# Token sums of a seven-product matrix scheme, made from resident token tiles instead of a second load, with a new instruction order

## The chip, the cores and the metric

The kernel runs on one core of one Trainium2 chip. TensorE (PE in the profile) multiplies matrices, VectorE (DVE) and ScalarE (ACT) work elementwise, GpSimd (POOL) and SyncE (SP) mostly issue DMA transfers. The metric is the device time of one execution in microseconds (us).

## The reference

Two branches work on the same 2048 tokens of 512 features and are mixed by a gate per token.

```python
g = sigmoid((x * gate_w).sum(-1, keepdims=True))
X = rfft2(x);  a = irfft2(X * (w_r + 1j * w_i), (2048, 512))     # a spectral filter
h = gelu(einsum("bsd,df->bsf", x, w1) + b1)                      # 512 -> 1792
b = einsum("bsf,fd->bsd", h, w2) + b2                            # 1792 -> 512
out = g * a + (1 - g) * b
```

Inputs are `x` (1, 2048, 512), `w1` (512, 1792), `w2` (1792, 512), the filter (2048, 257), all float32.

## The kernel before

Products in full float32 accuracy are made of rounded parts: an operand is split into a high part `h` (ScalarE copies it to the rounded type) and a low part `l` (VectorE subtracts `h` from the operand), and three products hh, hl, lh are added up on TensorE.

The tokens are taken in four classes `c` (position modulo 4, after a reordering), 512 tokens each. Classes 0 and 1 (`CA`) are the first half, 2 and 3 (`CB`) the second. The transform reads the tokens in 16 tiles of 128 x 512 (`xf`, tile `j` belongs to class `j % 4`); `forward(j)` folds a tile (`eo`, `w`), multiplies it with cosines and sines (`pd`, with the gate's weights in two extra columns of the table `cf`), splits the result (`zb`), and multiplies with twiddle tables `tf` (`py`). For the first half's classes `forward` also calls `split_x`, which writes the high and low part of the tile for the dense branch.

The dense branch takes 14 blocks of 128 hidden features. Blocks 0 and 1 of the first half are done with plain products (`ph`, in `plain`). All others go in pairs through `seven`: a 2 x 2 block product made with seven half-size products instead of eight (the banks `nu` and `ux`). It needs, besides some token blocks themselves, four sums and differences of them: with the four blocks 11, 12, 21, 22 (feature half by class) these are

```python
t1 = x12 - x11;  t3 = x22 - x12;  t2 = x22 - t1;  t4 = x21 - t2
```

and sums of weights (`spread_w`). After the activation the second product adds into the banks `po`, whose running sums `s` are kept in SBUF between groups of blocks.

In the kernel before, `spread_x("A")` loads the tokens of the first half a second time, in another layout (`xc`, 8 transfers of 256 KB into `xbA`), makes the four combinations with VectorE and splits each. `spread_x("B")` does so for the second half, where all seven forms are made from the loads.

The order of all work is a table, `ORDER`: the functions add numbered steps to a graph, and the steps are emitted in the order of the table, each to its engine's queue, which runs in order. A second table, `SLOTS`, says which buffer slot each tile takes. The numbers `more=` in the calls only describe costs for making the table and emit nothing.

Names in the order and the profile: `xA..` are split token forms of the first half, `xAt..` split combinations, `wa`, `wb` weights of blocks 0 and 1 and of the second product, `wA` weights of the seven-product scheme, `none` fillers that multiply zeros (nine at the start, five later), `gb` the gate spread to 512 columns per class.

Of the kernel before, what the change touches and what calls it, by code (L numbers as in the profile page):

```python
# [16 lines left out]
P = 128  # L17
# [332 lines left out]
def tile_kernel(ctx: ExitStack, tc: tile.TileContext, xt, xc, w1, w2, b1, b2, x0g, wf, wrev, out, consts):  # L350
# [193 lines left out]
    def new_forms(s, ks):  # L544
        FX.update(((s, k), buf("xhl", [P, 2, 2, 4 * P], F32R, f"x{s}{k}", parts=16, cls="xf")) for k in ks)

    def piece(b, hl, e, js=range(4)):
        return [(b, 8 * hl + 4 * i + j) for i in e for j in js]
# [18 lines left out]
    def forward(j):  # L567
# [13 lines left out]
        if c in CA:  # L581
            if j < 4:
                new_forms("A", ("11", "21") if c == 0 else ("12", "22"))
# [646 lines left out]
```

## Time and profile before

| | us |
|---|---|
| median of 3 runs | 358.27 |
| lowest and highest | 358.09, 358.92 |
| the profiled execution | 357.73 |
| its span, first to last instruction | 355.8 |

The page's rows give, for each engine, busy time, share of the span and number of instructions; PEld is TensorE's loading of weights, which overlaps the products. In rows of a timeline the first two numbers are start and duration in us, and a bracket at the end says how long the engine idled before and what ended the wait. Rows of stretches give for each engine the busy time and number of instructions, then TensorE's granted clock, the share of the DMA engines' time, and GB/s. The clock is at 1.00 in nearly all of the span.

### The profile page before, as it was taken

How to read it: one execution, taken by the hardware profiler on the slowest of the kernel's cores; microseconds unless marked ns; L12 is line 12 of the kernel's file. 1: busy time of each engine (PE TensorE's matmuls, PEld its weight loads, DVE VectorE, ACT ScalarE, POOL GpSimd, SP SyncE). 2: the span in 40 equal slices, each digit the busy share in tenths (PEclk: the TensorE clock that was granted, in tenths of full speed). 3: DMA queues.
4: the chain of work that ended last, by engine and by line, in shares of the span. 5: the costliest groups of instructions: out<-in, count | busy, mean ns of one | idle time of the engine just before them, and what ended most of it. 6: DMA issues, size and time to landing. Idle time of an engine off the chain costs nothing.

```text
span 355.8 us, 5738 instructions
## 1 busy us (share of the span) xinstructions
PE 348.8 (98%) x1770; PEld 294.8 (83%) x1770; DVE 323.1 (91%) x674; ACT 294.8 (83%) x612; POOL 38.7 (11%) x52
## 2 busy tenths in 40 slices
PE   7999999999999999999999999999999999999995
PEld 5988888888887888888888888878888888888884
DVE  5999997799999999999999999999989987779856
ACT  4989999999999984996678894589999899999510
POOL 1011101000102200010000400003000000021230
PEclk9999999999999999999999999999999999999999
DMA  7999868937798959997888954479403347345598
GB/s 230 371 270 321 158 191 287 242 125 212 184 277 210 332 115 294 357 272 236 282 274 224 220 110 99 131 261 207 135 7 104 96 134 234 123 106 133 111 201 272
DMA packets 47790, 72.47 MB, mean 204 GB/s; under 512 B 5648, under 2 KB 19472, under 8 KB 47760
## 3 DMA queue, kind: packets, MB, share of 16 engines
q1 hardware_dynamic: 40480, 61.51, 53.0%
q0 software_dynamic: 6848, 10.27, 18.5%
q10 hardware_dynamic: 432, 0.33, 0.3%
q8 instruction: 14, 0.23, 0.2%
q14 instruction: 16, 0.13, 0.1%
HBM read 52.55 MB, written 19.41 MB: 202 GB/s over the span
## 4 chain that ended last, share of the span: by engine, by line
PE 88%; DMA 5%; ACT 3%; DVE 1%; SPq 1%; issue 1%; DVEq 0%; ACTq 0%
PE po L415 39%; PE uxB L415 11%; PE uxA L415 9%; PE nuB L415 8%; PE nuA L415 7%; PE pz L415 4%; PE pa L415 3%; PE pd L415 3%; PE py L415 3%; DMA xbA<-in_xc 2%; DMA wb3l_raw<-in_w 2%; DMA xf<-in_xt 1%; PE ph L415 1%; ACT s L942 1%; DMA xf<-in_x0g 1%
## 5 line engine op out<-in xcount | busy, mean ns | idle before, releaser
L932 ACT ACTIVATE po<-s 128x512 f32<-128x512 f32 (+1 forms) x49 | 28.8, 594 | 8.0 <-DVE t L962 7.4
L424 ACT ACTIVATE s<-po 128x512 f32<-128x512 f32 x40 | 23.8, 597 | 13.1 <-PE po L415 12.8
L794 ACT ACTIVATE sw<-y,al 64x512 f32<-64x512 f32 x32 | 22.5, 718 | 0.5
L755 DVE TENSOR_TENSOR m<-y,wf 128x514 f32<-128x514 f32 x32 | 21.3, 688 | 0.6
L415 PEld LDWEIGHTS pd<-cf,w 128*128 128x128 f32 x128 | 17.7, 190 | 3.7 <-DVE cf L529 2.2
L415 PE MATMUL pd<-cf,w 128*128 128x129 f32 x128 | 19.2, 276 | 1.5 <-DVE cf L529 1.4
L415 PE MATMUL py<-zb,tf 128*128 128x258 f32 x96 | 19.6, 292 | 0.1
L409 POOL DMA_DIRECT2D w<-bacc x8 | 9.6, 1256 | 91.3 <-DVE w L842 81.0
L415 PEld LDWEIGHTS pz<-tg,pq 128*128 128x128 f32 x128 | 17.5, 190 | 1.9 <-issue 0.3
L415 PE MATMUL pz<-tg,pq 128*128 128x128 f32 x128 | 18.6, 275 | 0.0
L415 PEld LDWEIGHTS py<-zb,tf 128*128 128x128 f32 x96 | 15.5, 189 | 2.6 <-ACT zb L608 0.3
L801 DVE SCALAR_TENSOR_TENSOR pq<-y,al,sw 128x256 f32<-128x256 f32 x32 | 15.1, 478 | 2.8 <-ACT sw L794 1.9
L415 PE MATMUL nuB<-xB,wB0h 128*128 128x512 f32 x56 | 17.4, 391 | 0.0
L415 PE MATMUL pa<-zb,ci 128*128 128x256 f32 x96 | 16.2, 290 | 0.0
L415 PEld LDWEIGHTS pa<-zb,ci 128*128 128x128 f32 x96 | 14.0, 189 | 1.7 <-DVE zb L814 0.2
L612 DVE TENSOR_TENSOR zb<-pd,zb 128x256 fp32r<-128x256 f32 x32 | 13.2, 418 | 2.1 <-ACT logit L611 2.0
L415 PE MATMUL nuA<-xA,wA0h 128*128 128x512 f32 x48 | 14.9, 392 | 0.0
L942 ACT ACTIVATE s<-po,b2t 128x512 f32<-128x512 f32 x16 | 10.6, 689 | 5.0 <-PE po L415 5.0
L632 ACT ACTIVATE y<-pys 64x257 f32<-64x257 f32 x32 | 13.0, 416 | 0.8 <-DVE pys L629 0.3
L575 DVE TENSOR_TENSOR eo<-xf 128x256 f32<-128x256 f32 x32 | 12.6, 417 | 0.8 <-DMA xf<-in_x0g 0.4
L608 ACT ACTIVATE zb<-pd 128x256 fp32r<-128x256 f32 x32 | 11.9, 387 | 1.5 <-PE py L415 0.9
L814 DVE TENSOR_TENSOR zb<-pz,zb 128x512 fp32r<-128x512 f32 x16 | 10.9, 686 | 2.0 <-ACT zb L813 2.0
(532 smaller groups left out, 1225.3 us busy)
## 6 DMA issues: line engine op xcount, KB each, us to landing
wf<-in_wf SPq DMA_DIRECT2D x16, 257.0 KB, 3.9
xf<-in_xt SPq DMA_DIRECT2D x14, 256.0 KB, 5.0
tf<-tf SPq DMA_DIRECT2D x16, 192.0 KB, 3.6
wrA<-in_w SPq DMA_DIRECT2D x12, 256.0 KB, 5.5
xbA<-in_xc SPq DMA_DIRECT2D x8, 256.0 KB, 4.2
xbB<-in_xc SPq DMA_DIRECT2D x8, 256.0 KB, 4.8
bacc<-s SPq DMA_DIRECT2D x8, 256.0 KB, 2.8
w<-bacc POOLq DMA_DIRECT2D x8, 256.0 KB, 4.5
```

What stands on the lines that cost most here:

```text
L415: pe.matmul(ps, w, x, start=start, stop=stop, **more)
L424: a(lambda: act.activation(o.ap(), i.ap(), AF.Copy, scale=scale), n, [i], [o])
L575: v(lambda s=s, op=op: vec.tensor_tensor(eo.ap()[:, s], x.ap()[:, 0:2], x.ap()[:, 2:4], op=op), 256, [x], [(eo, s)])
L608: a(lambda c=c: act.activation(segs(xh, c), both(c), AF.Copy), 256, [ps[c]], [(xh, c)])
L612: v(lambda c=c: vec.tensor_tensor(segs(xl, c), both(c), segs(xh, c), op=ALU.subtract), 256, [ps[c], (xh, c)], [(xl, c)])
L632: a(lambda o=o, i=i: act.activation(Y[j].ap()[o:o + HP, 1], pys.ap()[i:i + HP, 1], AF.Copy), 257, [(pys, 1)], [(Y[j], 1 + k)], more=0.1)
L755: v(lambda mk=mk, k=k, y=y, w=w: vec.tensor_tensor(mk.ap(), y.ap(), w.ap()[:, k:k + 1, :ND].to_broadcast([P, 2, ND]), op=ALU.mult), 514, [ ...
L794: a(lambda sw=sw, y=y, o=o, i=i: act.activation(sw.ap()[o:o + HP], y.ap()[i:i + HP, ::-1, :HD], AF.Copy, scale=al.ap()[i:i + HP, 0:1]), 51 ...
L801: v(lambda sw=sw, pq_=pq_, y=y, j=j, k=k, op=op: vec.scalar_tensor_tensor(pq_.ap()[:, k], y.ap()[:, k, :HD], al.ap()[:, 1 + j:2 + j], sw.a ...
L814: v(lambda n=n, ps=ps: vec.tensor_tensor(zl.ap()[:, :, :, n], ps.ap(), zh.ap()[:, :, :, n], op=ALU.subtract), 512, [ps, (zh, n)], [(zl, n)])
L932: a(lambda ps=ps, n=n, o=o: act.activation(ps.ap(), o.ap()[:, n], AF.Copy), size, [o], [ps])
L942: a(lambda o=o, ps=ps, q=q: act.activation(o.ap(), ps.ap(), AF.Identity, bias=b2t.ap()[:, q:q + 1]), 600, [b2t, ps], [o])
```

## The change

`spread_x("A")` and its eight loads are gone. A new function `spread_a`, called from `forward` for each tile of class 1, makes the four combinations from the token tiles of class 0 and class 1 that the transform has loaded (kept in `RAW`), and splits them. The split forms of the first half are laid out in pairs: one buffer holds the high parts of two forms, another the low parts (`new_pair`), so that a split of a tile is one ScalarE instruction of 512 columns and one VectorE instruction of 512, where it was two and two of 256; two tiles of class 0 keep two ScalarE-side instructions of 256. The readers (`plain`, `seven`) take the forms through a function that says which buffer and part to read. `ORDER` and `SLOTS` are new throughout, which moves instructions on every engine.

```diff
-    def split_x(c, x, j1):
+    def split_x(pair, x, j1, first=False):
         n = slice(j1 * P, (j1 + 1) * P)
-        for k in range(2):
-            b = FX["A", ("11", "21")[k] if c == 0 else ("12", "22")[k]]
...
-                a(lambda b=b, k=k: act.activation(b.ap()[:, 0, :, n], x.ap()[:, 2 * k:2 * k + 2], AF.Copy), 256, i, o)
-        for k in range(2):
...
-            v(lambda b=b, k=k: vec.tensor_tensor(b.ap()[:, 1, :, n], x.ap()[:, 2 * k:2 * k + 2], b.ap()[:, 0, :, n], op=ALU.subtract), 256,
-              [*i, *piece(b, 0, range(2), [j1])], piece(b, 1, range(2), [j1]))
+        h, l = pair
...
+        else:
+            a(lambda: act.activation(h.ap()[:, :, n], x.ap(), AF.Copy), 512, [x, gate], where(h, range(2)))
+        v(lambda: vec.tensor_tensor(l.ap()[:, :, n], x.ap(), h.ap()[:, :, n], op=ALU.subtract), 512, [x, *where(h, range(2))], where(l, range(2)))
+
+    XP, RAW = {}, ([], [])
+
+    def spread_a(j1):
+        if j1 == 0:
+            XP["t1"], XP["t2"] = (new_pair("A", ks) for ks in (("t1", "t3"), ("t2", "t4")))
+        x, y = RAW[0][j1], RAW[1][j1]
+        t, u = (buf("w", [P, NQ, P], F32, f"xt{k}{j1}", parts=2, cls="xt") for k in range(2))
+
+        def less(o, n, i, k, w, m):
+            v(lambda: vec.tensor_tensor(o.ap()[:, 2 * n:2 * n + 2], i.ap()[:, 2 * k:2 * k + 2], w.ap()[:, 2 * m:2 * m + 2], op=ALU.subtract),
+              256, [i if i in (x, y) else (i, k), w if w in (x, y) else (w, m)], [(o, n)])
+
+        less(t, 0, y, 0, x, 0)
+        less(t, 1, y, 1, y, 0)
+        less(u, 0, y, 1, t, 0)
+        less(u, 1, x, 1, u, 0)
+        split_x(XP["t1"], t, j1)
+        split_x(XP["t2"], u, j1)
@@ in forward
-            split_x(c, x, j // 4)
+            split_x(XP[c], x, j // 4, c == 0 and j < 8)
+            RAW[c].append(x)
+            if c:
+                spread_a(j // 4)
@@ at the program's end
     group("A", 0)
-    spread_x("A")
@@ ORDER, first line of 110
-17 14 10 21 22 8 11 16 9 15 0 2 1 60 33 29 28 24 23 30 25 26 31 57 495 27 56 39 35 3 37 38 40 4 58 492 59 490 491 493
+10 21 22 14 8 18 20 19 17 11 9 0 1 2 3 4 5 6 7 32 60 59 33 513 514 528 106 16 15 28 29 23 24 31 26 56 55 25 57 30 27
```

TensorE's queue at the program's start, before:

```order
L415 MATMUL none_92<-zero_90 128x512 x9
L415 MATMUL pd01_124<-cf_86,w0_113 128x129
L415 MATMUL none_92<-zero_90 128x256
L415 MATMUL pd00_128<-cf_86,w0_113 128x129 x2
L415 MATMUL pd01_124<-cf_86,w0_113 128x129
L415 MATMUL none_92<-zero_90 128x256 x2
L415 MATMUL pd41_155<-cf_86,w4_133 128x129 x2
L415 MATMUL ph0_1_160<-xA11_104,wa1h_152 128x256 x2
L415 MATMUL ph0_1_160<-xA21_106,wa1h_152 128x256 x2
L415 MATMUL ph0_0_176<-xA11_104,wa0h_139 128x128 x2
```

The same queue and place, now:

```order
L414 MATMUL none_94<-zero_90 128x512 x9
L414 MATMUL none_94<-zero_90 128x256 x5
L414 MATMUL ph0_1_118<-xA11_21h_109,wa1h_116 128x256 x4
L414 MATMUL pd00_144<-cf_125,w0_133 128x129 x2
L414 MATMUL pd40_148<-cf_125,w4_140 128x129 x2
L414 MATMUL pd41_153<-cf_125,w4_140 128x129 x2
L414 MATMUL pd01_156<-cf_125,w0_133 128x129
L414 MATMUL ph0_0_164<-xA11_21h_109,wa0h_162 128x128 x4
L414 MATMUL py0_189<-zb1_76,tf0_167 128x258 x2
```

The five fillers come all at once, and four `ph` products of block 1 stand ahead of the first `pd`.

SyncE's queue of transfers at the start, before (`war` are the raw weights behind `wa`, `al` a small table of the last stage):

```order
L504 DMA xf4_84<-in_xt 128x256
L509 DMA cf_86<-cf 128x258
L504 DMA xf4_84<-in_xt 128x256
L509 DMA cf_86<-cf 128x258
L872 DMA war1_120<-in_w1 128x512
L869 DMA war0_135<-in_w1 128x256 x2
L534 DMA al_145<-al 128x17
L477 DMA xf8_147<-in_xt 128x512
L412 DMA tf4_183<-tf 128x384
L412 DMA tf0_188<-tf 128x384
L477 DMA xf12_193<-in_xt 128x512
```

and now:

```order
L503 DMA xf4_87<-in_xt 128x256 x2
L898 DMA war1_114<-in_w1 128x512
L533 DMA al_123<-al 128x17
L508 DMA cf_125<-cf 128x258 x2
L895 DMA war0_158<-in_w1 128x256
L411 DMA tf0_167<-tf 128x384
L895 DMA war0_158<-in_w1 128x256
L476 DMA xf12_171<-in_xt 128x512
L476 DMA xf8_173<-in_xt 128x512
L476 DMA xf9_181<-in_xt 128x512
L1048 DMA wrA4_185<-in_w1 128x512
```

`war1` and the second half of tile 4 moved ahead of the table `cf`, one `tf` moved ahead and the other behind, and a weight of the seven-product scheme (`wrA4`) came in among the token tiles.

ScalarE's queue in the opening, behind the first split of weights, before:

```order
L560 ACTIVATE xA21_106<-xf4_84 128x2x128
L560 ACTIVATE xA11_104<-xf0_78 128x2x128
L608 ACTIVATE zb1_80<-pd00_128 128x256
L560 ACTIVATE xA21_106<-xf8_147 128x2x128
L611 ACTIVATE logit_167<-pd00_128 128x2
L608 ACTIVATE zb1_80<-pd01_124 128x2x128
L560 ACTIVATE xA11_104<-xf8_147 128x2x128
```

and now:

```order
L634 ACTIVATE zb0_82<-pd40_148 128x256
L634 ACTIVATE zb1_76<-pd00_144 128x256
L568 ACTIVATE xA11_21h_109<-xf8_173 128x4x128
L637 ACTIVATE logit_209<-pd00_144 128x2
L634 ACTIVATE zb0_82<-pd41_153 128x2x128
L568 ACTIVATE xA11_21h_109<-xf12_171 128x4x128
L423 ACTIVATE wA0h2_240<-wrA4_185 128x512
L568 ACTIVATE xA12_22h_246<-xf9_181 128x4x128
L637 ACTIVATE logit_209<-pd41_153 128x2
L634 ACTIVATE zb1_76<-pd01_156 128x2x128
```

Splits of whole token tiles and of one weight block (`wA0h2`) now stand ahead of the copy of `pd01`.

More of the change, by code (lines that the diff above doesn't have):

```diff
@@ new lines, in new_form, with new_pair @@
+    def new_form(s, k):
+        b = buf("xhl", [P, 2, 2, 4 * P], F32R, f"x{s}{k}", parts=16, cls="xf")
+        FX[s, k] = lambda i, e: (lambda: b.ap()[:, i, e], [(b, 8 * i + 4 * e + j) for j in range(4)])
+    def new_pair(s, ks):
+        x = [buf("xhl", [P, 4, 4 * P], F32R, f"x{s}{'_'.join(ks)}{i}", parts=16, cls="xf") for i in "hl"]
+        for n, k in enumerate(ks):
+            FX[s, k] = lambda i, e, n=n: (lambda: x[i].ap()[:, 2 * n + e], [(x[i], 8 * n + 4 * e + j) for j in range(4)])
+        return x
@@ new lines, in split_x, with where @@
+    def split_x(pair, x, j1, first=False):
+        n = slice(j1 * P, (j1 + 1) * P)
+        h, l = pair
+        def where(b, ks):
+            return [(b, 4 * q + j1) for k in ks for q in (2 * k, 2 * k + 1)]
+        if first:
+            for k in range(2):
+                s, i = slice(2 * k, 2 * k + 2), [(x, k), gate]
+                if j1 == 0 and k:
+                    v(lambda s=s: vec.tensor_copy(h.ap()[:, s, n], x.ap()[:, s]), 256, i, where(h, [k]))
+                else:
+                    a(lambda s=s: act.activation(h.ap()[:, s, n], x.ap()[:, s], AF.Copy), 256, i, where(h, [k]))
+        else:
+            a(lambda: act.activation(h.ap()[:, :, n], x.ap(), AF.Copy), 512, [x, gate], where(h, range(2)))
+        v(lambda: vec.tensor_tensor(l.ap()[:, :, n], x.ap(), h.ap()[:, :, n], op=ALU.subtract), 512, [x, *where(h, range(2))], where(l, range(2)))
@@ L977, in last @@
                 store(lambda s=s, i=i, w=w: sp.dma_start(dst[:, n.start + i:n.start + i + w], t.ap()[:, s]), w / 2, o, [])
-    def put(b, e, x):
-        h, l = ((lambda i=i: b.ap()[:, i, e]) for i in range(2))
-        a(lambda: act.activation(h(), x.ap(), AF.Copy), 512, [x], piece(b, 0, [e]))
-        v(lambda: vec.tensor_tensor(l(), x.ap(), h(), op=ALU.subtract), 512, [x, *piece(b, 0, [e])], piece(b, 1, [e]))
-    def less(o, x, y):
-        v(lambda: vec.tensor_tensor(o.ap(), x.ap(), y.ap(), op=ALU.subtract), 512, [x, y], [o])
@@ L1072, in emit @@
                     for wi, xi in ((0, 0), (0, 1), (1, 0)):
-                        mm(o.ap(), w(wi, e), x.ap()[:, xi, e], start and k == 0, k == 5, skip_group_check=not start)
+                        mm(o.ap(), w(wi, e), x(xi, e)[0](), start and k == 0, k == 5, skip_group_check=not start)
                         k += 1
-            m(emit, 512, 6, [*bs, x], [o])
+            m(emit, 512, 6, [*bs, *[p for i in range(2) for e in range(2) for p in x(i, e)[1]]], [o])
         def plus(o, i, t):
@@ L1169, in tile_kernel @@
         stage4(c)
-    spread_x("B")
+    spread_x()
     for p in range(len(GROUPS[1])):
```

67 lines of the change are left out of this document (29 added, 38 removed), and 197 rows, old and new, of tables (ORDER, SLOTS).

## The prediction

> **What bounds the kernel now.** I read the page's engine shares first, then the busy time by stretches, then the chain that ended last, then the timelines of TensorE, VectorE, ScalarE and SyncE for the opening.
>
> ```profile
> span 355.8 us, 5738 instructions
> PE 348.8 (98%) x1770; PEld 294.8 (83%) x1770; DVE 323.1 (91%) x674; ACT 294.8 (83%) x612; POOL 38.7 (11%) x52
> 0.00:20.00 20.00, 17.43 (x117) 15.62 (x118) 15.69 (x50) 13.33 (x43) 2.66 (x13) 1.00 0.90 305
> 110.00:260.00 150.00, 149.87 (x661) 123.58 (x660) 145.69 (x279) 122.38 (x234) 17.93 (x21) 1.00 0.78 215
> 118.60 19.07 PE po L415 x84
> ```
>
> TensorE is busy 98% of the span. That alone proves little, since pipelined matmuls overlap in the records; the two other lines do. In the stretch from 110 to 260 us it issued 661 records in 150 us, 0.227 us each, and the chain has 84 `po` matmuls in 19.07 us, again 0.227. So TensorE never waited there: 0.227 us is its own pace for 512 columns, and no order of the other engines can make this stretch shorter, only longer. VectorE had 145.69 of 150 us busy beside it, so it is the engine with the least to spare (4.3 us).
>
> The Trainium skill ("Trainium Kernel Development and Optimization", Best Practices) says to judge the distance to the limit by the share of weight loading, not by matmul busy time. By that, 83% would leave some 60 us to win. The trace differs: in the stretch without a single wait weight loading is also only 123.58 of 150 us (82%), so 83% is here what a full TensorE looks like, and I go by the pace of the matmuls.
>
> What can be won lies at the two ends. Of TensorE's opening:
>
> ```profile
> 1.05 4.21 PE L415 MATMUL none<-zero 128*128 128x512 f32 x9 [1.05 <-DVE zero L483]
> 6.70 0.49 PE L415 MATMUL pd<-cf,w 128*128 128x129 f32 x2 [1.44 <-DVE cf L529]
> 14.12 0.65 PE L415 MATMUL ph<-xA,wa1l 128*128 128x256 f32 x4
> 14.60 0.28 PE L415 MATMUL py<-zb,tf 128*128 128x258 f32 x1
> 21.27 0.40 PE L415 MATMUL py<-zb,tf 128*128 128x258 f32 x2
> 21.51 0.62 PE L415 MATMUL ph<-xA,wa1h 128*128 128x512 f32 x2
> 27.10 1.05 PE L415 MATMUL pd<-cf,w 128*128 128x129 f32 x8
> 27.91 0.61 PE L415 MATMUL py<-zb,tf 128*128 128x258 f32 x3
> ```
>
> From starts to starts: four 256-column matmuls take 0.48 us (14.12 to 14.60), so 0.12 each; two of 258 columns 0.24, so 0.12 each; eight `pd` records, which are four fold instructions, 0.81, so 0.20 a fold. Half of 0.12 for 128 columns is an estimate. Before the first 512-column `ph` matmul at 21.51 the kernel before has, behind the nine warm-ups, 5 fillers (0.60), 44 `ph` of 256 (5.28), 8 of 128 (0.48), 23 `py` (2.76) and 20 folds (4.05): 13.2 us. With 1.05 and 4.21 that is 18.4, so 3.1 us of the opening were waiting.
>
> **The change, part by part.**
>
> *TensorE's work.* Counted by tile and width in the two orders, every group is the same (`po`, `nu`, `ux`, `ph`, `py`, `pd`, `pz`, `pa`, fillers). Cost 0; the span can move only by waits.
>
> *Loads removed.* Eight `xbA` loads of 256 KB leave SyncE's queue.
>
> ```profile
> L993 SPq DMA_DIRECT2D xbA<-in_xc x8: 328/426/777, 11.6 to 43.0; - x8
> L981 ACT ACTIVATE xAt<-xbA x8: 622/648/673, 37.6 to 53.4; 128x512 fp32r<-128x512 f32 x8
> 10.00:20.00 10.00, 9.93 (x81) 9.56 (x81) 9.93 (x29) 8.49 (x30) 0.89 (x1) 1.00 1.04 371
> ```
>
> At 371 GB/s their 2.1 MB are 5.7 us of transfer, issued from 11.6 to 43.0 us, and 8 x 0.43 us of issue. Nothing in the trace is named as waiting for them, so I take 0 for the removal itself. What is next in the queue may land sooner by up to these 5.7 us; the bound on the gain is the waiting that exists, 3.1 us.
>
> *ScalarE and VectorE.* ScalarE splits eight token tiles with 15 instructions of 256 and, in the removed code, eight of 512; now 3 and 14. Twelve of 256 go, six of 512 come.
>
> ```profile
> 10.98 0.37 ACT L628 ACTIVATE pys<-py 128x257 f32<-128x257 f32 x1
> 11.25 0.74 ACT L560 ACTIVATE xA<-xf 128x256 fp32r<-128x256 f32 x2
> 11.89 0.15 ACT L611 ACTIVATE logit<-pd 128x2 f32<-128x2 f32 x1
> 327.44 1.28 DVE L814 TENSOR_TENSOR zb<-pz,zb 128x512 fp32r<-128x512 f32 x2
> 328.64 0.41 DVE L842 TENSOR_TENSOR w<-u 128x256 f32<-128x256 f32 x1
> ```
>
> Two of 256 take 0.64 - 0.32 each; one of 512 does not exceed the 0.65 us of the `xAt` row, about 0.52 without overlap with its neighbour. Twelve times 0.32 is 3.8, six times 0.52 is 3.1: 0.7 us saved on an engine that idles 61 us. I take 0 (bounds: nothing to 0.7 us gained). VectorE had 17 of 256 and 16 of 512 in these two functions and has 17 and 16 now: 0, but about 10 us of it (16 x 0.335 and 8 x 0.60) stand no longer behind a load at 29 to 55 us; they are free to run once the eight token tiles are in.
>
> *The opening's order.* This is the term that I count. The rows for it:
>
> ```profile
> 5.71 0.42 ACT L560 ACTIVATE xA<-xf 128x256 fp32r<-128x256 f32 x1 [2.55 <-DMA xf<-in_xt]
> 6.66 0.63 ACT L424 ACTIVATE wa1h<-war 128x512 fp32r<-128x512 f32 x1 [0.53 <-DMA war<-in_w]
> 10.66 0.42 ACT L560 ACTIVATE xA<-xf 128x256 fp32r<-128x256 f32 x1 [0.35 <-DMA xf<-in_xt]
> 4.39 0.76 DVE L575 TENSOR_TENSOR eo<-xf 128x256 f32<-128x256 f32 x2 [0.40 <-DMA xf<-in_x0g]
> 5.07 0.22 DVE L521 TENSOR_TENSOR g<-g 128x2 f32<-128x2 f32 x2
> 6.48 0.16 DVE L529 COPY cf<-g 128x4 f32<-128x4 f32 x1
> 6.55 0.42 DVE L575 TENSOR_TENSOR eo<-xf 128x256 f32<-128x256 f32 x1
> ```
>
> In the kernel before, TensorE stands until VectorE has written the gate columns into `cf` (6.48) and starts `pd` 0.22 us later. In the new order the weights `war1` are issued two places sooner, ahead of both `cf` halves, and four `ph` matmuls stand ahead of the first `pd`. `war1` landed at 6.66 with 1035 KB issued up to it; now it is 777 KB, 258 KB less, 0.7 us at 371 GB/s: 5.96. ScalarE's split adds about 0.55, so the four `ph` run from 6.6 to 7.1, where TensorE idled. `cf` is now behind 1044 KB instead of 779, 0.7 us later, but at 6.48 VectorE came to the COPY from other work without idling, so it had landed by then, and now by 7.2 at the latest. VectorE's own queue has one `eo` and one `w` more ahead of the COPY and puts it at 4.39 + 0.68 + 5 x 0.335 + about 0.3 for tiny ones = 7.0; `pd` starts at about 7.25. From there I add rows in queue order, each step at the later of its own engine and its input:
>
> - Seven folds (1.4) and four `ph` of 128 (0.24) end at 8.9, when ScalarE has copied both first `pd` banks (twice 0.27 behind the fourth fold).
> - VectorE, never idle from 4.39, has the low parts of tokens and weights ready at 9.25 (`xA..l`), 9.85 (`wa1l`) and 11.1 (`wa0l`); TensorE reaches them at 9.3, 10.0 and 11.2, so waits of at most 0.15 each.
> - `tf4` is the next late one: tile 12 landed at 10.66 with 2196 KB issued; `tf4` has 2964 KB, 2.1 us later, 12.7. TensorE is there at 12.55.
> - The low part of tile 8 (VectorE, 13.7) costs about 0.35; then all inputs are ahead until the first 512-column `ph`, whose last input, the low part of tile 1, VectorE ends at 18.1.
>
> So that matmul starts at about 18.25. Ahead of it stand now 5 fillers, 44 and 8 `ph`, 12 `py` and 16 folds: 0.60 + 5.28 + 0.48 + 1.44 + 3.24 = 11.0, with 5.26 in front 16.3. Waiting is 1.95 instead of 3.1: **1.1 us gained**. Bounds: 3.1 gained if no wait were left; on the other side, tile loads that land 1 us later than this rate are 1 us lost, so 0 gained at least down to 1 us lost.
>
> *The middle and the end.* The whole order is new, so waits between 50 and 340 us can come or go. From 110 to 260 none can go. I take 0, with 0.5 us gained and 2 us lost as bounds: the lower by the few tenths of waiting elsewhere, the upper by half of VectorE's 4.3 idle us. The last block is the same kind of chain (two half-size `po`, VectorE, an output transfer), and its rows show VectorE one tile behind TensorE:
>
> ```profile
> 350.72 0.41 DVE L962 SCALAR_TENSOR_TENSOR t<-gb,po 128x256 f32<-128x256 f32 x1
> 352.50 0.29 DVE L971 TENSOR_TENSOR t<-y,t 128x128 f32<-128x128 f32 x1
> 352.82 0.35 ACTq L975 DMA_DIRECT2D out<-t  x1
> ```
>
> In the new order the same eight VectorE instructions close it: 0.
>
> *Sum.* The profiled execution took 357.73 us, its span 355.8 and 1.9 around it. 357.73 - 1.1 = 356.6. The median of the runs is 358.27, 0.54 above that execution, so I predict 357.2 us, 0.3% faster. A change of 0.2% (0.7 us) is about what can be told from none.
>
> **Rivals.**
>
> *The lead is eaten again (no change).* The first `po` needs `wb1l`, which ScalarE writes and a POOL transfer then adds to.
>
> ```profile
> 20.58 0.85 POOL L409 DMA_DIRECT2D wb1l<-in_w  x1 [2.46 <-ACT y L628]
> 29.42 0.48 PE L415 MATMUL po<-g_1h,wb1h 128*128 128x512 f32 x1
> wA0l<-in_w POOLq DMA_DIRECT2D x6, 256.0 KB, 5.2
> ```
>
> The kernel before issued it at 20.58 and TensorE came at 29.42, 8.8 us later. In the new order I put ScalarE's part at 19.5 and TensorE's arrival at 18.25 + 8.1 = 26.3: at 5.2 us a transfer it lands 1.6 us early, but one that takes 7.9 eats the lead. The same happens if VectorE, at 97% from 110 us on, meets TensorE at the same time as before. Time: 358.3, or 357.6 if half is left.
>
> *ScalarE stops for tokens and weights (slower).* ScalarE's opening queue now has six 512-wide token splits, each behind a load, and `wA0h2`, whose weights TensorE needs only after 38 us, ahead of the copy of bank `pd01` that the `py` at about 14.4 needs. At the rate above `wA0h2`'s load (2516 KB) lands at 11.6 and that copy is done at 13.0, 1.4 us early. Each us of landing beyond that is a us of TensorE. The rows speak for some of it (ScalarE's waits of 2.55, 0.53 and 0.35 us on loads), against it that the stretch ran at 371 GB/s. It decides from 3.2 us of lateness on (1.4 + 1.1 + 0.7): 359.0 and up, 359.5 at 3.7.
>
> *TensorE's clock falls back (slower).* The nine warm-ups ran at 0.47 us for 512 columns against 0.227 later. The new order spends the five fillers at once, so two holes of about 0.7 and 0.15 us follow. If the pace halved again for the 4.2 us of the warm-ups, 2.1 us are lost: 359.3. Against it: the kernel before idles 1.44 us at the same place and the clock column is 1.00. The Trainium skill ("TensorE: Matmul & The Clock Gate", What's actually happening) gives an idle window of about 3.4 us for the fall; by that rule the holes are too short, and the trace agrees as far as 1.44 us goes.
>
> **How the numbers follow.** Opening gain kept: 0.57, of it 356.3 to 357.5. Eaten: 0.27 (357.6 to 358.9). ScalarE late: 0.09; clock: 0.02; some wait in the new middle of 2 us: 0.05 (all above 359.0). So faster 0.57, same 0.27, slower 0.16. The range that leaves out 2 in 10 takes 356.2 (one more us of the 3.1) to 359.2.
>
> **What would show it.** Right: first `pd` near 7.25 behind four `ph`; first 512-column `ph` before 19 us; no `xbA`; from there the 0.227 pace. Wrong: that matmul at 19.4 or later; a wait of TensorE on `wb1l` near 26 us; a stretch between 110 and 260 us with fewer than 4.4 records per us.

## The result, and the profile after

| | before | after |
|---|---|---|
| median of 5 runs each, us | 358.27 | 360.42 |
| lowest and highest | 357.42, 358.92 | 360.13, 360.70 |
| the profiled execution | 357.73 | 360.31 |
| its span | 355.8 | 358.5 |

The changed kernel takes 1.0061 of the time before (95% interval 1.0044 to 1.0078): 0.6% slower, where 0.3% faster was predicted.

The page's head, and the chain that ended last, by engine. Of before only the chain was not yet shown; it comes first.

```profile
PE 88%; DMA 5%; ACT 3%; DVE 1%; SPq 1%; issue 1%; DVEq 0%; ACTq 0%
```

```profile
span 358.5 us, 5674 instructions
PE 349.6 (98%) x1770; PEld 294.3 (82%) x1770; DVE 323.4 (90%) x674; ACT 294.2 (82%) x606; POOL 38.8 (11%) x52
PE 19%; ACT 12%; DVE 5%; issue 1%; ACTq 0%; DVEq 0%
```

Busy times hardly changed: TensorE has the same 1770 matmuls, ScalarE six instructions less. The chain did change. It ran through TensorE for 88% of the span; now it can be followed back for only 37%, a third of that on ScalarE.

To see where 2.7 us of span came in, I set the starts of successive matmuls against the pace of a run without a wait (0.227 us for 512 columns, 0.119 for 258, 0.1185 for 256, 0.060 for 128, 0.111 for each record of the full float32 products `pd` and `pz`, and 0.24 for each of the two of `pown`). What is beyond it is TensorE's loss; the sum of the paces is 342.1 us in every kernel here, and the 1.05 us ahead of the first matmul are left aside. By the time at which the loss falls, and with the distance from the last matmul's start to the span's end, in us:

| | 0-20 | 20-50 | 50-120 | 120-200 | 200-246 | 246-331 | later | last to end |
|---|---|---|---|---|---|---|---|---|
| before | 4.84 | 0.81 | 1.00 | -0.09 | 0.39 | 1.26 | 0.10 | 4.45 |
| after | 4.93 | 0.59 | 1.85 | -0.12 | 0.45 | 2.02 | 0.14 | 5.60 |

So three places lost: 50 to 120 us (0.85), 246 to 331 us (0.76) and the end (1.15). The opening, where the prediction saw its gain, is level. Its loss includes the fillers at the program's start: the first products run at about half pace (0.43 us for 512 columns), which makes 1.9 us of the 4.84 and 1.4 of the 4.93.

**The opening.** TensorE's timeline after:

```profile
1.05 4.23 PE L414 MATMUL none<-zero 128*128 128x512 f32 x14 [1.05 <-DVE zero L482]
6.26 0.74 PE L414 MATMUL ph<-xA_21h,wa1h 128*128 128x256 f32 x4 [0.98 <-ACT wa1h L423]
7.57 1.83 PE L414 MATMUL pd<-cf,w 128*128 128x129 f32 x14 [0.57 <-DVE cf L528]
13.36 0.48 PE L414 MATMUL py<-zb,tf 128*128 128x258 f32 x2
14.67 0.74 PE L414 MATMUL ph<-xA_21l,wa0h 128*128 128x256 f32 x4 [0.37 <-DVE xA_21l L569]
19.30 0.39 PE L414 MATMUL ph<-xA_22h,wa0h 128*128 128x512 f32 x1
```

The four `ph` did go into the hole ahead of the first `pd` (6.26, forecast 6.6). But the first 512-column `ph` came at 19.30, not at 18.25. With the 16.3 us of work that the prediction counts ahead of it, 3.0 us were waiting, as 3.1 before. The work was in truth shorter: the pace doubled at about 4 us, and all 14 fillers took 4.23 us, where the nine alone had taken 4.21 before. So the waiting itself rose by some 0.5 us. VectorE and ScalarE show how the lead went:

```profile
3.97 0.29 DVE L564 CAST xA_21h<-xf 128x256 fp32r<-128x256 f32 x1 [2.97 <-DMA xf<-in_x0g]
7.35 0.17 DVE L528 COPY cf<-g 128x4 f32<-128x4 f32 x1
13.59 0.42 DVE L638 TENSOR_TENSOR zb<-pd,zb 128x256 fp32r<-128x256 f32 x1 [0.47 <-ACT logit L637]
13.93 0.68 DVE L569 TENSOR_TENSOR xA_21l<-xf,xA_21h 128x512 fp32r<-128x512 f32 x1
17.13 1.90 DVE L569 TENSOR_TENSOR xA_22l<-xf,xA_22h 128x512 fp32r<-128x512 f32 x3
```

```profile
12.02 0.63 ACT L423 ACTIVATE wA0h<-wrA 128x512 fp32r<-128x512 f32 x1
12.54 0.63 ACT L568 ACTIVATE xA_22h<-xf 128x512 fp32r<-128x512 f32 x1
13.06 0.17 ACT L637 ACTIVATE logit<-pd 128x2 f32<-128x2 f32 x1
13.11 0.39 ACT L634 ACTIVATE zb<-pd 128x256 fp32r<-128x256 f32 x1
13.37 0.19 ACT L637 ACTIVATE logit<-pd 128x2 f32<-128x2 f32 x1
```

VectorE started 0.27 us later than before (3.70 to 3.97), and stood 0.47 us, ahead of its step at 13.59, for the gate's columns, which ScalarE copied at 13.37, behind the weight block `wA0h2` and token tile 9. The low part of tile 8 stands behind that step in VectorE's queue: it ended at 14.62 (forecast 13.7), and the low parts of class 1 at 19.03 (forecast 18.1). The `py` at 13.36 cost another 0.27 us: its table `tf4` landed at 13.22 (forecast 12.7).

The new order has one more dependency, which this execution hides. `SLOTS` now gives `wa1h` the buffer of `zero`, which the fillers read (before, each had its own), so ScalarE can write `wa1h` only when the last filler is done. Here the fillers were done at 5.28 and ScalarE came at 5.60. In 11 of the other 14 executions of the new order below ScalarE waited for them; in seven the fillers ran at half pace to their end, the wait was 0.77 to 1.18 us, and the four `ph` came at 7.04 to 7.11. The row of the first of these (stores alone):

```profile
6.42 0.63 ACT L423 ACTIVATE wa1h<-war 128x512 fp32r<-128x512 f32 x1 [1.18 <-PE none L414]
```

No run gives `wa1h` a buffer of its own, so what this costs at the end of the opening is not shown.

**The stretch from 50 to 120 us**, in the view by stretches (time; then busy time and instructions of TensorE, its weight loading, VectorE, ScalarE, GpSimd; clock, DMA share, GB/s), before and after:

```profile
50.00:120.00 70.00, 70.00 (x357) 58.97 (x356) 62.84 (x131) 68.41 (x161) 7.67 (x9) 1.00 0.80 223
50.00:120.00 70.00, 69.89 (x360) 58.41 (x360) 59.56 (x124) 67.56 (x164) 7.72 (x9) 1.00 0.76 211
```

Two waits for ScalarE stand out after: 0.38 us are lost at 89.4 to 89.6, where three `pd` follow each other, and 0.17 at 57.9 to 58.3. The rest of the 0.85 is in pieces of 0.1 us and less. ScalarE was no fuller there than before (67.56 of 70 us, 68.41 before), so a larger amount of its work is not what made these waits.

**The stretch from 246 to 331 us**, in the view by stretches, before and after, and ScalarE's waits there by what ended them, before and after:

```profile
246.00:331.00 85.00, 84.96 (x472) 73.09 (x471) 75.54 (x157) 80.19 (x137) 3.58 (x3) 1.00 0.44 122
```

```profile
246.00:331.00 85.00, 84.67 (x461) 71.83 (x460) 77.45 (x163) 81.91 (x141) 6.53 (x7) 1.00 0.41 105
```

```profile
ACT s L424 <- PE po L415: 1.1, 2, 0.8
ACT od L424 <- PE pa L415: 0.8, 3, 0.4
```

```profile
ACT od L423 <- PE pa L414: 0.2, 1, 0.2
ACT s L423 <- PE po L414: 0.2, 1, 0.2
```

(Of ScalarE's waits before, two of five rows are shown.) TensorE issued 461 matmuls there where it had issued 472. ScalarE had waited for TensorE, 2.4 us in seven places; now it waits 0.4 in two. TensorE's loss is in four waits: at 277.5, 280.5, 299.0 and 318.9 us, 0.94 us of the 2.02, where before a single one of 0.19 stood. Three of them were for ScalarE, the one at 299.0 for a `pq` of VectorE. ScalarE seems to be the engine that has no time left. The `sw` products of the inverse transform (ScalarE's, by line: count, shortest, median and longest in ns, first and last start) show what changed:

```profile
L794 ACT ACTIVATE sw<-y,al x32: 701/722/728, 243.3 to 322.8; 64x512 f32<-64x512 f32 x32
```

```profile
L820 ACT ACTIVATE sw<-y,al x32: 703/722/726, 253.4 to 322.9; 64x512 f32<-64x512 f32 x32
```

The same 32 began 10 us later and had to be done by the same time.

**The end.** SyncE's queue in the last 20 us, before and then after, with GpSimd's accumulating transfers of after (a row's duration is issuing, with the waits within the group):

```profile
338.55 2.40 SPq L848 DMA_DIRECT2D out<-w  x2
345.94 0.94 SPq L977 DMA_DIRECT2D out<-t  x2
350.83 1.98 SPq L977 DMA_DIRECT2D out<-t  x3
```

```profile
337.58 2.67 SPq L1003 DMA_DIRECT2D out<-t  x2
347.77 0.90 SPq L874 DMA_DIRECT2D out<-w  x2
348.76 2.11 SPq L1003 DMA_DIRECT2D out<-t  x3
353.11 2.04 SPq L1003 DMA_DIRECT2D out<-t  x3
338.80 2.39 POOL L408 DMA_DIRECT2D w<-bacc  x2 [7.20 <-ACT od L423]
```

`w` is a block of the result of class 0 or 1: `inverse` makes it, an accumulating transfer adds `bacc` (the other branch), SyncE stores it. In the new order the store of `w100`, a block of class 0, stands at the head of SyncE's queue from 340.2 us on and goes out at 347.77, when its accumulating transfer has landed (issued at 339.52, landed at 347.75). The store of `w000`, landed at 343.85, stands behind it. So 12 stores, 2.6 MB, went out from 347.77 on, and DMA was still full from 354 to 356 us, behind the last matmul's start at 352.91:

```profile
354.00:356.00 2.00, 0.00 (x0) 0.00 (x0) 0.33 (x2) 0.00 (x0) 0.00 (x0) 0.86 1.06 372
```

In the kernel before, the same two microseconds moved 6 GB/s. VectorE's last step ended 1.45 us after the last matmul's start in both.

### The profile page after: what moved, and what is told of

Read it like the earlier page. It is cut to its first block, busy times and chain, and to the rows that moved or that the text cites. A ratio compares the mean times of both kernels' runs of the same rounds, so it can differ in the third digit from the quotient of the medians.

```text
span 358.5 us, 5674 instructions
## 1 busy us (share of the span) xinstructions
PE 349.6 (98%) x1770; PEld 294.3 (82%) x1770; DVE 323.4 (90%) x674; ACT 294.2 (82%) x606; POOL 38.8 (11%) x52
## 5 line engine op out<-in xcount | busy, mean ns | idle before, releaser
L414 PE MATMUL py<-zb,tf 128*128 128x258 f32 x96 | 20.5, 295 | 0.1
L414 PE MATMUL pd<-cf,w 128*128 128x129 f32 x128 | 18.8, 277 | 0.7 <-DVE cf L528 0.6
L414 PE MATMUL pz<-tg,pq 128*128 128x128 f32 x128 | 18.1, 275 | 0.1
L601 DVE TENSOR_TENSOR w<-eo 128x256 f32<-128x256 f32 x32 | 13.2, 422 | 0.2
```

Of the source, the lines that this page charges most:

```text
L414: pe.matmul(ps, w, x, start=start, stop=stop, **more)
L601: v(lambda s=s, op=op: vec.tensor_tensor(w.ap()[:, s], eo.ap()[:, :, 0], eo.ap()[:, :, 1], op=op), 256, [eo], [(w, s)])
```

## The experiments

My theory after reading the traces: three places of the new order cost the time, one by one (the end through SyncE's queue, ScalarE's stretch, the opening through ScalarE); the removed loads are worth nothing. The rivals stand in the expectations. The edits move steps in the table `ORDER` of the changed kernel, unless another base is named; they are shown as the queues of the engines concerned. Each measured number is the time as a share of the kernel before, which was run beside it, with the 95% interval; the unedited changed kernel stands at 1.0061 (1.0044 to 1.0078).

**Stores alone.**

```diff
 SyncE: out<-w111, out<-t210, out<-t320,
-  out<-w100, out<-w000, out<-t200, out<-t230, out<-t300, ...
+  out<-t300, out<-w000, out<-w100, out<-t200, out<-t230, ...
 VectorE: second step of t300 from behind the first of t200 to behind w101
```

> The changed kernel with one edit in the last 20 us: SyncE's queue issues the stores of w000 and of t300 ahead of the store of w100 (which waits 8 us, until 347.77, for an accumulating transfer), and VectorE's second step of t300 moves into its idle time at 343 us so that t300 is ready. Theory Q (SyncE's in-order queue holds back half a MB that is ready, and the last stores then find 0.5 MB, 1.4 us at 370 GB/s, ahead of them): the first store after 347.7 is w100 alone, the distance from the last matmul's start to the span's end falls from 5.6 to about 4.5 us, and the time falls by 1.0 us, ratio to before about 1.003. Rival A (the DMA engines are busy from 341 to 356.5 us without a gap because the accumulating transfers take that long, so the order of the stores changes nothing): the distance stays at 5.3 to 5.6 us, ratio 1.005 to 1.006.

Measured: 1.0024 (1.0009 to 1.0039). Last matmul to end 4.47 us in place of 5.60; the four other executions below that keep this end had 4.84 to 5.30.

**Accumulating transfers alone.**

```diff
 VectorE:
-  v00, w000 (half), y, zb, zb, t210, w100 (half), w000 (half), ..., w100 (half)
+  v00, w000 (half), w000 (half), zb, zb, y, w100 (half), w100 (half), t210
 GpSimd: each w<-bacc straight behind its second half
```

> The changed kernel with one edit: VectorE finishes w000 at about 335.8 and w100 at 337.7 us, by moving two steps of each together and one step of y behind them, so that their two accumulating transfers are issued at about 336 and 338 us in place of 338.8 and 339.5; SyncE's order stays. Rival A (the end is set by the accumulating transfers, which start 1 to 2.4 us later than in the kernel before): all later landings move 1.5 to 2.5 us earlier, the distance from the last matmul to the end falls from 5.6 to about 4.5 us, ratio about 1.003. Theory Q (the queue order alone) expects part of that too, since the wait of w100's store ends sooner with its transfer; if that store still goes out after 346 us the distance stays at 5.3 or more. TensorE is expected to see nothing of it.

Measured: 1.0040 (1.0028 to 1.0052); last to end 4.49 us. GpSimd issued at 336.19 and 338.36, and the store of `w100` went out early enough:

```profile
342.87 2.07 SPq L874 DMA_DIRECT2D out<-w  x2
347.35 2.14 SPq L1003 DMA_DIRECT2D out<-t  x3
```

So both theories hold a half: either letting the ready stores pass or making the late one ready removes the backlog, and they are not added up (with both, 4.06 to 4.50 us in eight kernels below). By its time alone the second edit is not told from the unedited kernel, since the intervals overlap.

**Neighbours swapped.**

```diff
 TensorE, at 277.54, 280.54, 288.73 and 318.86:
-  pa (waits), po or ux
+  po or ux, pa
 and at 298.96:
-  pz11 (waits), pz15
+  pz15, pz11
```

> The changed kernel with five pairs of neighbours swapped in TensorE's queue between 277 and 321 us: at each place where TensorE waited for ScalarE or VectorE (277.54, 280.54, 288.73, 298.96, 318.86 us; 0.27, 0.12, 0.06, 0.27, 0.29 us, each followed by some 0.1 us on the next matmul) the product behind goes first. Theory O (these waits are single late inputs made by the new order, with other work ready behind): they vanish, TensorE's last matmul starts about 1.0 to 1.4 us earlier, ratio about 1.003. Rival S (ScalarE and VectorE are the pace there, so a wait that is removed comes back at the next step): under 0.4 us gained, ratio 1.005 to 1.006, with new waits of like size nearby.

Measured: 1.0037 (1.0022 to 1.0052). The loss from 246 to 331 us was 1.89 us after 2.02: the rival S was right, the waits came back (0.20 at 279.23, 0.35 at 290.47, 0.18 at 323.01). The ratio is better than 0.13 us explains; its interval overlaps that of the unedited kernel, and I read nothing from it.

**Opening.**

```diff
 ScalarE:
-  wA0h2, xA..h (tile 9), logit, zb<-pd01, logit<-pd40
+  zb<-pd01, logit<-pd40, wA0h2, xA..h (tile 9), logit
 TensorE:
-  py4 x2, ph (high), ph (low, tile 8), py4, py0 x2, ph, pd120, py0, ph<-wa0l
+  ph (high), py4 x3, py0 x2, ph (low, tile 8), ph, ph<-wa0l, pd120, py0
```

> The changed kernel with an edit of the opening: ScalarE copies bank pd01 and the gate's columns of pd40 before it splits the weight block wA0h2 and the token tile 9 (VectorE waited 0.47 us for that at 13.1), and TensorE takes four ready steps (a ph of the high parts, three py) ahead of the two that waited for a tf table and for the low part of tile 8 (0.27 and 0.53 us lost). Theory W (ScalarE's work for later stages, put ahead of what the fold needs, is what ate the predicted 1.1 us): VectorE runs without the 0.47 us wait, the first 512-column ph starts at 18.5 to 18.8 in place of 19.30, ratio about 1.004. Rival V (VectorE's amount of work alone sets the opening: it ends the low parts of class 1 at 19.03 us whatever TensorE does): the start stays above 19.1. Rival L (landings set it, as tiles 8 and 12 land): TensorE waits at the same two places as before.

Measured: 1.0029 (1.0017 to 1.0042). The first 512-column `ph` started at 19.00, later than the 18.5 to 18.8 expected, with a first `ph` at 7.11 behind slow fillers. In the executions whose first `ph` came at 7.04 to 7.11 it started at 19.50, 19.79, 20.07 and 20.26 without this edit, and at 18.65, 19.00 and 19.77 with it: 0.8 us sooner on average, with overlap. The low part of tile 8 ended at 13.91 in place of 14.62. VectorE's wait for gate columns did not go, as the theory has it: it came back at 15.04 (0.46 us), behind that low part. What ScalarE's order and what TensorE's gives was not separated. The profiled execution (361.05 us) was the slowest of 12 (median 359.28) and shows where a lead can go:

```profile
207.44 0.21 ACT L778 ACTIVATE wf<-edges 128x4 f32<-128x4 f32 x1 [3.98 <-DMA wf<-in_wf]
224.81 0.21 ACT L778 ACTIVATE wf<-edges 128x4 f32<-128x4 f32 x1 [3.36 <-DMA wf<-in_wf]
227.84 0.73 PE L414 MATMUL uxB<-xBt,wBth 128*128 128x512 f32 x2 [1.58 <-ACT uxB L423]
```

ScalarE patches four columns of a filter tile as soon as it lands, with all its other work queued behind; late landings became 1.6 us of TensorE's time. In the unedited kernel these two waits were 2.37 and 1.57 us.

**One-row products on GpSimd.** `sw`'s row 64 has a scale of its own: 16 ScalarE instructions of 1 x 512, 0.63 us each.

```diff
-  act.activation(sw.ap()[HP:HP + 1], y.ap()[HP:HP + 1, ::-1, :HD], AF.Copy, scale=...)
+  nc.gpsimd.tensor_scalar(sw.ap()[HP:HP + 1], y.ap()[HP:HP + 1, ::-1, :HD], ..., None, op0=ALU.mult)
```

> The changed kernel with one edit: the 16 one-row products of the inverse transform (sw<-y of 1 x 512, 0.63 us each, 9.8 us of ScalarE between 246 and 331 us, where it idles 0.8 us) are made by GpSimd, which idles there. Theory S (ScalarE has no time left in that stretch, in the kernel before it had 3.6 us, and so TensorE meets late copies there whatever the order of neighbours): ScalarE idles some 9 us there, TensorE's losses from 270 to 330 us fall from 2.0 to 1.2 us or less, the last matmul starts 0.8 to 1.0 us earlier, ratio 1.003 to 1.004. Rival D (the waits are the length of single chains, pz to zb to pa, not the amount of ScalarE's work): losses stay at 1.8 us or more, ratio 1.005 to 1.006. Rival G (GpSimd takes over 2 us for a row, or slows VectorE beside it): ratio above 1.006.

Measured: 1.0056 (1.0036 to 1.0076). The same edit in the kernel before, as a control:

> The kernel before with the same edit, as a control: 16 one-row products of the inverse transform on GpSimd in place of ScalarE. TensorE loses 1.15 us from 270 to 330 us there, of it 0.3 us at one wait for VectorE and the rest fixed costs of switching from full float32 products. Theory S: ScalarE had 3.6 us to spare, so at most 0.3 us gained, ratio 0.999 to 1.000. Rival G: slower, ratio above 1.001.

Measured: 1.0019 (1.0004 to 1.0035). Rival G has the mechanism in both: a row takes GpSimd 1.68 us, and VectorE slows beside it. The ratio above 1.006 that it named for the changed kernel did not come; the one for the kernel before did. TensorE's waits turned from ScalarE to VectorE. ScalarE's share could not be read from this.

**All repairs**: stores, accumulating transfers, opening, and the two patches put behind three ScalarE steps each; with the rows on GpSimd, and with the rows left on ScalarE.

> The changed kernel with all repairs: the stores and accumulating transfers of the last 20 us as in the two runs on them, the opening's edit, the one-row products on GpSimd, and two patches of the filter tiles (ScalarE waited 2.4 and 1.5 us for their loads at 206 and 222 us) put behind three steps that have their input. Theory (tail 1.1, ScalarE's stretch 0.8 to 1.0, opening 0.5 to 0.9, the wait at 214 to 238 us 0.3): together 2.6 to 3.3 us under the 360.4 of the changed kernel, 357.1 to 357.8, ratio 0.997 to 0.999. Rival (gains ahead of 228 us are eaten where TensorE meets ScalarE): 2.0 us gained, 358.4, ratio 1.000.

> As the run with all repairs, but the one-row products stay on ScalarE. Theory S: 0.8 to 1.0 us slower than that run, TensorE's losses from 270 to 330 us at 2.0 us, ratio 0.999 to 1.002. Rival D: the two do not differ by more than 0.3 us.

Measured: 1.0017 (1.0003 to 1.0032) with GpSimd, 1.0009 (0.9996 to 1.0021) without. The repairs give back most of the 0.61%; the patches alone were not tried. Both forecasts missed: the first run should have come below 0.999, and the second be 0.8 to 1.0 us slower than the first, where it was not slower.

**Rows left out**, on the second of these, with the kernel before as a control:

```diff
-  a(lambda sw=sw, y=y, j=j: act.activation(sw.ap()[HP:HP + 1], ...), 512, [y], [(sw, 1)], more=0.13)
+  a(lambda: None, 512, [y], [(sw, 1)], more=0.13)
```

> The kernel with the repairs of tail, opening and filter patches (the one-row products on ScalarE took 1.0009 of the time before, with GpSimd 1.0017); here the 16 one-row products of the inverse transform are left out altogether, so that one row of the filter branch is wrong and neither ScalarE (9.8 us less) nor GpSimd (1.68 us each, beside slower VectorE steps) carries them. Theory S (ScalarE's 81.9 busy of 85 us from 246 to 331 us is what TensorE's waits there come from): TensorE's losses from 270 to 330 us fall from 2.0 to 1.0 to 1.3 us, ratio 0.997 to 0.999. Rival D (single chains): losses 1.8 us or more, ratio 1.000 to 1.002.

> The kernel before with the 16 one-row products of the inverse transform left out (one row of the filter branch is wrong): the control for the same omission in the new order, where it took 1.3 us off. Theory S (the new order, not the omission as such, made ScalarE the limit): TensorE's losses from 270 to 330 us fall from 1.15 to 0.7 us or so, ratio 0.9985 to 0.9995. Rival E (ScalarE limits that stretch in both orders alike): 1.0 us or more gained, ratio 0.996 to 0.9975.

Measured: 0.9971 (0.9954 to 0.9988) in the new order, 0.9986 (0.9970 to 1.0002) in the order before. The stretch of the repaired kernel, the same without the rows, and the control:

```profile
246.00:331.00 85.00, 84.73 (x462) 71.89 (x461) 77.36 (x163) 81.76 (x140) 6.52 (x7) 1.00 0.40 105
```

```profile
246.00:331.00 85.00, 85.00 (x473) 73.62 (x471) 78.82 (x167) 72.84 (x125) 6.54 (x6) 1.00 0.44 109
```

```profile
246.00:331.00 85.00, 85.00 (x475) 73.69 (x474) 76.05 (x158) 70.63 (x122) 3.58 (x3) 1.00 0.44 122
```

With 9 us less on ScalarE TensorE issues 473 matmuls again, and its loss falls from 2.04 to 0.71 us; in the control from 1.26 to 0.94. So in the new order these 9 us of ScalarE's work cost 1.3 us there, in the order before 0.3: TensorE waits for ScalarE, and the new order made it so. Whether that is by the amount of work is not shown. The omission also takes a step out of each chain from `y` over `sw` and `pq` to `pz`, and a run below speaks against the amount alone.

**More swaps** on the repaired kernel: the five from above, and a `po` ahead of three `pd` at 88 us.

> The kernel with the repairs of tail, opening and filter patches (one-row products on ScalarE), with the five swaps of neighbours between 277 and 321 us and one more: a po ahead of three pd at 88 to 90 us, where TensorE lost 0.27 and 0.18 us behind a bank that ScalarE was still reading. Theory S: the swap at 88 us gains 0.3 us since there is slack behind it, the five gain 0.2 at most; TensorE's losses in the whole fall from 9.6 to about 9.1 us, ratio 1.000. If all six waits go: 8.3 us, ratio 0.997.

Measured: 1.0020 (1.0006 to 1.0033); the loss rose from 9.6 to 10.3 us, where 9.1 or 8.3 was expected. From 50 to 120 us it rose from 1.82 to 2.36: the `po` now waited for ScalarE itself (0.45 us lost at 88.64), and a `py` for another copy of ScalarE (0.41 at 101.00). So a swap on TensorE wins nothing there either; the next thing that it meets is ScalarE again.

**The fault put into the kernel before.**

```diff
 SyncE (before): out<-t320, out<-t300,
-  out<-w111, out<-w000, out<-t220, out<-t310, out<-w100, ...
+  out<-w100, out<-w111, out<-w000, out<-t220, out<-t310, ...
```

> The kernel before with one store moved: in SyncE's queue the store of w100, whose accumulating transfer lands at 344.5 us, stands ahead of those of w111 and w000, which are ready at 338.5 and 340.6. So the fault found at the end of the changed kernel is put into the one before, with the same half MB held back. Theory Q: the distance from the last matmul's start to the span's end rises from 4.45 to 5.0 to 5.6 us, ratio 1.002 to 1.003; TensorE's own losses stay. Rival A (busy transfer engines alone, no matter in which order): 4.45 to 4.7 us, ratio 1.000.

Measured: 1.0040 (1.0020 to 1.0059); last to end 5.77 us in place of 4.45.

```profile
344.15 1.50 SPq L848 DMA_DIRECT2D out<-w  x3
354.00:356.00 2.00, 0.00 (x0) 0.00 (x0) 0.00 (x0) 0.00 (x0) 0.00 (x0) 0.70 0.81 276
```

Three stores leave together at 344, and the transfers run on past 354 us. One store's place in one queue is enough for a loss as large as that of the changed kernel's end.

**Loads given back.**

```diff
+  sp.dma_start(again[i], xc[i // 4, i % 4])    # behind eight SyncE steps between 12 and 45 us
```

> The changed kernel with the traffic of the removed loads given back: eight transfers of 256 KB of the same tokens in SyncE's queue, issued between 12 and 45 us, into DRAM that nothing reads. Theory (nothing ever waited on those loads, and the removal was worth nothing): ratio 1.005 to 1.007 as the changed kernel. Rival (their 2.1 MB, 5.7 us at 371 GB/s, delayed what stood behind them, and the removal was worth up to 1.1 us that other losses hide): ratio 1.008 or more, with the added time as waits of TensorE between 20 and 50 us.

Measured: 1.0064 (1.0041 to 1.0088), as the changed kernel; the loss from 20 to 50 us is 0.58 after 0.59. It was 5.88 us up to 20 us, the highest of the six executions with that opening (4.68 to 5.88). The trace gives another reason for it than loads: TensorE's products ran at half pace until 10.5 us here (0.21 us for 256 columns at 7.5 to 8.1).

**Rows on VectorE** where it has time, on the repaired kernel: six, nine, and three with a sooner copy; then the copy alone.

```diff
+  if j in (6, 10, 14, 11, 9, 5): v(... vec.tensor_scalar(...)) ahead of the pq that reads it
 nine: (6, 10, 14, 3, 11, 7, 9, 5, 13); three: (11, 9, 5)
 three, and copy alone: VectorE g_2l and ScalarE uxB11<-uxB10 two steps sooner
```

> The kernel with the repairs of tail, opening and filter patches, with six of the 16 one-row products of the inverse transform (tiles 6, 10, 14, 11, 9, 5) made by VectorE just ahead of the step that reads them, so that ScalarE carries 3.8 us less between 246 and 331 us and idles about 4 us as in the kernel before; VectorE idles 7.5 us there and carries about 3 us more. The result is whole. Theory S (what ScalarE has to spare in that stretch decides): TensorE's losses from 270 to 330 us fall from 2.0 to 1.2 us or less, ratio 0.998 to 0.9995. Rival V (VectorE becomes the engine without time, as when GpSimd worked beside it): losses 1.7 us or more, ratio 1.000 to 1.002.

> As the run with six rows on VectorE, but nine (tiles 6, 10, 14, 3, 11, 7, 9, 5, 13): ScalarE carries 5.7 us less, VectorE about 4.5 us more of the 7.5 it idles. Theory S: no more than 0.2 us better than with six. Rival V: TensorE's waits turn to VectorE's steps (pq, zb, tg), 0.3 us or more slower than with six.

Measured: six 1.0030 (1.0013 to 1.0048), nine 1.0052 (1.0034 to 1.0070). Six was slower than either forecast. From 280 to 331 us six rows did what they should (loss 1.0 us in place of 1.5), but two of them, at 276.27 and 278.06 just ahead of the `zb` that TensorE waited for, made VectorE late:

```profile
280.25 0.74 PE L414 MATMUL pa<-zb,ci 128*128 128x256 f32 x4 [1.15 <-DVE zb L845]
```

> The kernel with the repairs of tail, opening and filter patches, with only three one-row products on VectorE (tiles 11, 9 and 5, where VectorE itself waited for ScalarE at 287 and 293 us), and at 237 us the copy of bank uxB1 on ScalarE two steps sooner (with VectorE's g_2l that frees the bank two steps sooner too; TensorE lost 0.35 and 0.11 us there). The result is whole. Theory (ScalarE's spare time decides where VectorE has some): losses from 280 to 330 us as with six rows, 1.0 in place of 1.5 us, without the wait of 1.3 us at 280, and 0.4 us gained at 237; last matmul 0.9 us earlier than with the repairs alone, ratio 0.9975 to 0.9995. Rival: the waits move on to the next steps of either engine, ratio 1.000 to 1.002.

> As the run before, without the three rows: the repairs and the sooner copy of uxB1 at 237 us alone. Theory: 0.4 us gained at 237 us is kept, since behind it TensorE runs to 277 us without a wait only if ScalarE keeps up; ScalarE has 0.8 us of idle time from 246 to 331 us, so I expect half of it to come back as waits there: losses from 270 to 330 us at 2.0 to 2.3 us, ratio 0.9995 to 1.001.

Measured: 0.9998 (0.9986 to 1.0010) and 0.9998 (0.9984 to 1.0013). The wait at 237 us went in both; the gain did not grow further with three rows (loss from 246 to 331 us 2.11 and 2.18 us), as the rival has it. With the three rows ScalarE was busy 80.27 of the 85 us, as in the kernel before (80.19), and TensorE still lost 2.11 us where that one lost 1.26: so the amount of ScalarE's work alone does not make the loss, and the place of its steps or VectorE beside it (79.07 us, 75.54 before) must take part; this was not tested. These are the best of the new order with the whole result: level with the kernel before, no faster.

## Why the prediction was wrong, point by point

- *TensorE's work, loads removed, ScalarE's and VectorE's amounts: 0.* Right. The counts are the same, and the traffic of the loads given back changed nothing that can be measured.
- *Opening 1.1 us gained.* Failed: 0.1. The step that failed is "VectorE, never idle from 4.39": the step that stood at 4.39 began at 4.66, and VectorE idled 0.47 us from 13.12. These two make 0.7 of the 0.9 us by which the low part of tile 8 was late. The first is the landing of this one execution (that step began at 4.2 to 4.6 in the other runs of the new order), the second is the order's: 0.47 to 1.23 us in five of the six executions of this opening. I had ScalarE's late copy (done at 13.0, measured 13.50) and weighed it against the `py` at 14.4, 1.4 us away; I did not look at who else waits for that queue. VectorE's low part for `pd40` needs ScalarE's copy of the gate's columns, and the low part of tile 8 stands behind it. Over six executions with this opening TensorE lost 4.7 to 5.9 us up to 20 us, over four with the order before 4.8 to 5.9, over nine with the edited opening 4.3 to 5.4 (means 5.3, 5.2, 4.6). So on average some 0.7 us was there to be had, and the new order spent it. Part of the spread within each group is the moment at which TensorE's pace doubles, from 4 to 10.5 us after the start: the fillers alone lose 1.4 to 2.4 us by it.
- *Middle 0, between 0.5 gained and 2 lost.* Failed as a term put at 0: 0.85 was lost at 50 to 120 us and 0.76 at 246 to 331, inside the bounds together. The upper bound was taken from VectorE's idle time, and that was the wrong engine: of TensorE's larger waits there, all but the one at 299.0 us were for ScalarE, whose work I had put at 0 because it idles 61 us of the whole span. "From 110 to 260 none can go" was not quite so: the kernel before had lost 0.41 us at 235.8 to 236.1, the changed one lost 0.33 at 237.8 to 238.2, and the last two runs took that away. With 659 matmuls in place of 661 the stretch stands at 4.39 per us, just under the sign of 4.4, since the 0.47 us lost around `pown` moved into it from 108 us to 112.
- *The end 0, "the same eight VectorE instructions close it".* They do, at the same distance. The step that failed is that nothing behind them was costed, though the term speaks of an output transfer: the held store made 1.15 us in the profiled execution, 0.4 to 1.15 in the five executions with that end.
- *Rivals.* `wb1l` was never waited for. Behind the two holes (0.98 and 0.57 us) the `ph` and `pd` ran at full pace, so the pace did not fall back; that it can rise late, at 10.5 us with the loads given back and at 10.1 with the fault in the kernel before, no rival had, and the clock column shows 1.00 there too. ScalarE did not stop for `wA0h2` (its copy began at 12.02 without a wait), but that this block stood ahead of what the fold needs was the right place to look, with VectorE as the victim in TensorE's stead. Some wait in the new middle had a chance of 0.05; it comes nearest to what happened, and the end was in none.

Sum by the table: 0.09 - 0.22 + 0.85 - 0.03 + 0.06 + 0.76 + 0.04 + 1.15 = 2.7 us of span, in one execution of each kernel. Not settled: what made the `sw` products begin 10 us later. VectorE, whose `y` they read, was busy 88.98 us from 20 to 120 us where it had been busy 92.15, with 3.8 us of waiting for ScalarE's `y` copies where it had been 0.6; that this is the cause was not tested. Nor are the smaller pieces from 50 to 120 us explained.

## What to carry to other kernels

Read an engine's spare time by stretches and not from its share of the span: ScalarE at 82% had 3 us left in the 85 that mattered, and its place in the chain counts beside the amount. Where an order is rewritten, follow each queue that runs in order, the transfer queues to the last store: one store put ahead of its input holds all that stand behind it. A waiting step must be weighed against everything queued behind whoever waits for it, not only against TensorE. Where a table of buffers is rewritten too, look for new pairs that share one.

## What the runs showed of the hardware

An operation on one partition is not cheap, and differs by engine: 512 elements of one row took 0.63 us on ScalarE, 0.42 on VectorE and 1.68 on GpSimd. While GpSimd worked on these rows, some of VectorE's steps slowed whose operands both come from SBUF (the longest `y<-v` took 831 ns), and none that read PSUM (`zb` at most 692); first the changed kernel, then the one with rows on GpSimd:

```profile
L840 DVE TENSOR_TENSOR zb<-pz,zb 128x512 fp32r<-128x512 f32 x14 | 9.4, 687 | 2.3 <-ACT zb L839 2.1
L868 DVE TENSOR_TENSOR y<-v 128x256 f32<-128x256 f32 x7 | 2.7, 421 | 0.0
```

```profile
L823 POOL TENSOR_SCALAR sw<-y 1x512 f32<-1x512 f32 x16 | 26.9, 1679 | 35.9 <-ACT sw L820 35.0
L840 DVE TENSOR_TENSOR zb<-pz,zb 128x512 fp32r<-128x512 f32 x14 | 9.4, 684 | 1.1 <-ACT zb L839 1.0
L868 DVE TENSOR_TENSOR y<-v 128x256 f32<-128x256 f32 x7 | 3.1, 479 | 0.0
```

The Trainium skill ("SBUF — State Buffer", SBUF: two separate sides) says that a VectorE operation with two SBUF inputs and a GpSimd operation that reads SBUF exclude each other for a whole instruction. The traces agree as far as the kinds go: 421 to 479 ns on average for the one, 687 to 684 for the other; not every step of the first kind beside a row was longer.

An accumulating transfer of 256 KB took 5.1 to 8.2 us from issue to landing at the end of the changed kernel, where plain stores took 3.5 to 4.3.
